# Attention heads between projection pairs: a hand-laid order on TensorE, and a low part formed from PSUM

## The chip, the cores and the metric

The kernel runs on one core of one Trainium2 chip. The metric is the device time of one execution in microseconds; three runs of the kernel before are compared by their median. TensorE (PE in the profile) multiplies matrices into PSUM, ScalarE (ACT), VectorE (DVE) and GpSimd (POOL) work elementwise, and SyncE (SP) issues the transfers. Each engine takes its own instructions in order and waits for others by semaphores.

## The reference

```
scores = scale * q @ k.T                       # 8 batches, 8 heads, 576 positions, 64 wide
mask_local   = (rel >= 0) & (rel < 32)         # heads 0 to 3
mask_strided = (rel >= 0) & (same position modulo 32)   # heads 4 to 7
attn = exp(scores - max) / (sum + 1e-9)
x = (attn @ v), heads side by side             # 4608 tokens x 512
h = max(x @ w_in, 0)                           # 512 -> 2048
out = (h * h) @ w_out                          # 2048 -> 512
```

All inputs and the output are float32.

## The kernel before

The 4608 tokens are worked off in 12 chunks of 384. For each chunk there are two parts: the attention that makes its x, and the two projections.

**Projections.** A slot is one sixteenth of the hidden width of one chunk, so there are 16 slots j in a chunk and 192 slots s in all. `up(c, j)` makes 128 hidden values for the 384 tokens: twelve matmuls of 384 columns into one bank of PSUM (line 430), because each product is split into high and low parts (high by high, high by low, low by high) over four pieces of the input width. The bank is one of three, in turn. ScalarE then applies Relu and Square in place (435, 436) and casts to the high part `gh` (437); VectorE subtracts that from the bank to get the low part `gl` (438). Both have two buffers, so `gh` of slot s waits until the down projection of slot s-2 has read its own. `down(c, j)` adds the slot's part of the output with nine matmuls of 512 columns (line 450) into three banks that stay open through the chunk; after the chunk's last slot they are copied out and stored. The slots are traced as up(s), then down(s-2), so two ups lie ahead of each down.

**Strided heads.** For the heads 4 to 7 of the later chunks GpSimd multiplies (380, 402) and VectorE sums (381, 403). TensorE takes no part.

**Local heads.** For the chunks 2 to 11, each of the four heads 0 to 3 is a generator, `pe_head`, with six stages, a `yield` after each:

- stage 0: two loads, q with k, and v (208, 209)
- stage 1: ScalarE casts k and q to a high part, GpSimd subtracts for the low part (214 to 217)
- stage 2: four score matmuls in two banks (231); VectorE adds the mask and takes the minimum (235, 223)
- stage 3: exponent on ScalarE (240), sums and reciprocal on VectorE, scaling (245 or 248)
- stage 4: v is split in parts (251, 252); VectorE transposes the probabilities (256) into `p_t`; ScalarE casts their high part (262) and VectorE subtracts for the low part (263), into `px`
- stage 5: four output matmuls in two banks (273); per bank ScalarE copies one third part out (276), VectorE adds the two others (277, 278); then x is cast and its low part made (280, 281)

The banks of the heads are `ps3` and `ps4`, dealt in turn by one counter, two calls in stage 2 and two in stage 5:

```
    def bank(nm):
        return psum(3 + next(turn) % 2, f"{nm}{u}")
```

A new tile of a bank waits until every reader of the tile before it is done.

**What sets the order.** Each engine's instructions are put in order when the program is built, by a planner that works with its own costs: it places what is ready by its own clock, with the order of the code as a guide. `tc.issue_after(ins)` ties the instructions traced inside it to come after `ins` on the engine of `ins`, in order of issue only, and binds no other engine. In the kernel before, the heads' stages for chunk c+1 are traced between the slots of chunk c by the function `local` and the counters `dl`, `fl`, and the planner chooses where their matmuls come among the projections. Chunks 0 and 1 have their local heads from another function, `pe_pair`. Weights are loaded and converted during chunk 0.

Of the kernel before, what the change touches and what calls it, by code (L numbers as in the profile page):

```python
# [17 lines left out]
HL = H // 2  # L18
# [5 lines left out]
TC = 384  # L24
WP = 512
NCHUNK = NT // TC
NFT = DF // P
# [57 lines left out]
def attn_moe(ctx: ExitStack, tc, qk_l, v_l, qk_d, v_d, qk_p, v_p, f_s, q_s, k_s, v_s, w_in, w_out, masks, eye, out):  # L85
# [107 lines left out]
    def pe_head(c, h):  # L193
        u = f"{c}_{h}"

        def bank(nm):
            return psum(3 + next(turn) % 2, f"{nm}{u}")

        def buf(pl, nm, n, tag, **kw):
            return pl.tile([P, n], F32, name=f"{nm}{u}", tag=tag, **kw)  # L200

        qk, vp = buf(lraw, "qk", TC + KC, "qk"), buf(lraw, "v", NW * D, "v")
        e = buf(lpool, "e", 512, "e")
        qr, kr = qk[:, :TC], qk[:, TC:]
        vr = vp.rearrange("p (w d) -> p w d", d=D)
        kw, wins = KW, [(at, 0 if qc == 0 else 1) for _, qc, at in windows(c)]
        nk = wins[-1][0] + KW
        nc.sync.dma_start(out=qk[:, : TC + nk], in_=qk_l[c, h, :, : TC + nk])
        last["s"] = nc.sync.dma_start(out=vp, in_=v_l[c, h])
        yield  # L210

        qx = lpool.tile([P, TC], F32R, name=f"qx{u}", tag="qh", bufs=1)
        kx = lpool.tile([P, 2, KC], F32R, name=f"kx{u}", tag="kx", bufs=1)
        nc.scalar.copy(kx[:, 0, :nk], kr[:, :nk])
        nc.gpsimd.tensor_sub(kx[:, 1, :nk], kr[:, :nk], f32(kx[:, 0, :nk]))  # L215
        nc.scalar.copy(qx, qr)
        nc.gpsimd.tensor_sub(qx[D:], qr[D:], f32(qx[D:]))
        yield
        nmax = small.tile([P, 2 * NW], F32, name=f"nm{u}", tag="nm")
        ssum = sums[h % 3]  # L220
        rs = small.tile([P, 2 * NW], F32, name=f"rs{u}", tag="rs")[:, :NW]
        cut = lambda w: slice(w * kw, (w + 1) * kw)
        reduce = lambda w, src, m: nc.vector.tensor_tensor_reduce(  # L223
            out=e[:QC, cut(w)], in0=src, in1=m, scale=-SCALE, scalar=3.0e38,
            op0=ALU.add, op1=ALU.min, accum_out=nmax[:QC, w : w + 1],
        )
        for a in range(0, NW, 2):
            s_ps = bank(f"s{a}")
            for w in (a, a + 1):
                k0 = wins[w][0]  # L230
                nc.tensor.matmul(s_ps[:QC, 256 * (w - a) : 256 * (w - a + 1)], qx[:, w * QC : (w + 1) * QC], kx[:, :, k0 : k0 + kw], start=True, stop=True)  # L231
            sv = s_ps[:QC].rearrange("p (w t k) -> p w t k", w=2, t=2)
            m = wins[a][1]
            ev = e[:QC, a * kw : (a + 2) * kw].rearrange("p (w k) -> p w k", w=2)
            nc.vector.tensor_add(ev, sv[:, :, 1, :], mask_sb[:QC, m : m + 2, :])
            for w in (a, a + 1):
                reduce(w, sv[:, w - a, 0, :], e[:QC, cut(w)])
        yield
        for w in range(NW):
            nc.scalar.activation(e[:QC, cut(w)], e[:QC, cut(w)], AF.Exp, bias=nmax[:QC, w : w + 1], scale=-1.0, accum_out=ssum[:QC, w, :1])  # L240
        nc.vector.tensor_reduce(out=rs[:QC], in_=ssum[:QC, :NW], op=ALU.add, axis=AX.X)
        nc.vector.reciprocal(rs[:QC], rs[:QC])
        if h != HL - 1:
            for w in range(NW):
                nc.scalar.mul(e[:QC, cut(w)], e[:QC, cut(w)], rs[:QC, w : w + 1])  # L245
        else:
            ew = e[:QC, : NW * kw].rearrange("p (w k) -> p w k", k=kw)
            last["g"] = nc.gpsimd.tensor_mul(ew, ew, rs[:QC].unsqueeze(2).broadcast_to([QC, NW, kw]))
        yield
        vx = lpool.tile([P, NW, 2, D], F32R, name=f"vx{u}", tag="vx", bufs=1)  # L250
        nc.scalar.copy(vx[:, :, 0, :], vr)
        nc.gpsimd.tensor_sub(vx[:, :, 1, :], vr, f32(vx[:, :, 0, :]))
        pt = p_t[h % 2]
        for r in range(QC // STR):
            for k in (r, r + 1):
                nc.vector.transpose(  # L256
                    out=pt[STR * k : STR * (k + 1), :, STR * r : STR * (r + 1)],
                    in_=e.rearrange("p (w k) -> p w k", k=KW)[STR * r : STR * (r + 1), :, STR * k : STR * (k + 1)],
                )
        src = pt.rearrange("p w q -> p (w q)")  # L260
        px = lpool.tile([P, 2, TC], F32R, name=f"px{u}", tag="px")
        nc.scalar.copy(px[:, 0, :], src)
        nc.vector.tensor_sub(px[:, 1, :], src, f32(px[:, 0, :]))  # L263
        yield
        x = x_tiles(c)
        par, hp = D * (h % 2), h // 2

        src = e[par : par + D, :TC]
        for a in range(0, NW, 2):
            o_ps = bank(f"o{a}")  # L270
            for w in (a, a + 1):
                sl = slice(w * QC, (w + 1) * QC)
                nc.tensor.matmul(o_ps[:, 2 * QC * (w - a) : 2 * QC * (w - a + 1)], vx[:, w].rearrange("p t d -> p (t d)"), px[:, :, sl], start=True, stop=True)  # L273
            ov = o_ps[:, : 4 * QC].rearrange("p (w t q) -> p w t q", w=2, t=2)
            part = src[:, a * QC : (a + 2) * QC].rearrange("p (w q) -> p w q", w=2)
            nc.scalar.copy(part, ov[D:, :, 0, :])
            nc.vector.tensor_add(part, ov[:D, :, 1, :], part)
            nc.vector.tensor_add(part, ov[:D, :, 0, :], part)
        dst = [x["l", s][par : par + D, hp, :] for s in "hl"]
        last["a"] = nc.scalar.copy(dst[0], src)  # L280
        last["g"] = nc.gpsimd.tensor_sub(dst[1], src, f32(dst[0]))
        yield
# [137 lines left out]
    def up(c, j):  # L420
        x = xt[c]
        p, o = divmod(j, 2)
        ph = psum(j % 2 if c == 0 else (c * NFT + j) % 3, f"h{c}_{j}")
        n = 0
        for kt in range(4):
            kind, kk = "ls"[kt // 2], kt % 2
            xh, xl = x[kind, "h"][:, kk, :], x[kind, "l"][:, kk, :]
            wsl = slice(kt * 256 + o * P, kt * 256 + (o + 1) * P)
            for w, xx in ((wi[p][0], xh), (wi[p][0], xl), (wi[p][1], xh)):
                nc.tensor.matmul(ph[:, :TC], w[:, wsl], xx, start=n == 0, stop=n == 11)  # L430
                n += 1
        gh = gpool.tile([P, TC], F32R, name=f"gh{c}_{j}", tag="gh")
        gl = gpool.tile([P, TC], F32R, name=f"gl{c}_{j}", tag="gl")
        g = ph[:, :TC]
        nc.scalar.activation(g, g, AF.Relu)  # L435
        nc.scalar.activation(g, g, AF.Square)  # L436
        nc.scalar.copy(gh, g)  # L437
        nc.vector.tensor_sub(gl, g, f32(gh))  # L438
        g_tiles[c, j] = gh, gl

    def down(c, j):
        gh, gl = g_tiles.pop((c, j))
# [4 lines left out]
        for t in range(NTT):  # L447
            sl = slice(t * P, (t + 1) * P)
            for k, (g, w) in enumerate(((gh, wo[p][0]), (gh, wo[p][1]), (gl, wo[p][0]))):
                nc.tensor.matmul(y_ps[c][t], g[:, sl], w[:, wsl], start=j == 0 and k == 0, stop=j == NFT - 1 and k == 2)  # L450
        if j == NFT - 1:
            for t in range(NTT):
                y = ypool.tile([P, DM], F32, name=f"ysb{c}_{t}", tag="ysb")
                (nc.scalar.copy if t == 1 else nc.vector.tensor_copy)(y, y_ps[c][t])
                nc.sync.dma_start(out=out[c * TC + t * P : c * TC + (t + 1) * P, :], in_=y)


    def run(gen):
# [37 lines left out]
        return pe_pair(c, pr, local, *b, bank, place % 3)  # L496

    def local(c):
        if c < NPLAIN:
            heads = [pair_at(c, pr, True, pr, "34") for pr in range(2)]  # L500
            turns = (0, 0, 1, 0, 1, 0, 0, 1, 1, 1)
        else:
            heads = [pe_head(c, h) for h in range(HL)]

            turns = [0] * 3
            for h in range(HL):
                turns += [h] + [h + 1] * (3 if h + 1 < HL else 0) + [h] * 2
        for h in turns:
            next(heads[h])
            yield  # L510

    ungated = convert()

# [50 lines left out]
    NS = NCHUNK * NFT  # L564
    for s in range(NS + 2):
        c, j = divmod(s, NFT)
        if s < NS:
            up(c, j)
        if s >= 2:
            down(*divmod(s - 2, NFT))  # L570
        if c == 0:
            for _ in range(WRATE):
                if next(weights, "end") != "end":
                    weights_end = {e: last[e] for e in "agsv"}
        if c + 1 < NCHUNK:
            if j == 0:
                lo, st = local(c + 1), strided(c + 1)
                if c == 0:
                    lo, st = behind(heads_end, lo), behind(heads_end, st)
                if c == 1:  # L580
                    lo, st = behind(weights_end, lo), behind(weights_end, st)
                cost = sum(2 * sum(range(i0 + 1, i1 + 1)) + 10 for _, i0, i1, _ in ranges(c + 1))
                dl = ds = 0
            fl, fs = ((j + 1) / n for n in SPREAD[min(c, 1)])
            while dl < fl * (10 if c + 1 < NPLAIN else 6 * HL) and next(lo, "end") != "end":
                dl += 1
            while ds < fs * cost:
                k = next(st, "end")
# [82 lines left out]
```

## Time and profile before

| | us |
|---|---|
| median of three runs | 903.63 (903.14 to 903.86) |
| profiled execution | 902.66 |
| its span, first to last instruction | 900.8 |
| TensorE busy | 886.3 (98%) |
| VectorE busy | 669.5 (74%) |
| GpSimd busy | 693.4 (77%) |
| ScalarE busy | 564.4 (63%) |

The mean granted clock of TensorE is 0.982 of full speed over the span. Rows of the profile are read like this. A row of the timeline has start, length, engine, line, operation, what is written from what, and how many such instructions were merged; in brackets the idle time before and what ended it. A row of the groups has busy time and mean length in ns, then the engine's idle time in front of the group. A row of the windows has the stretch, its length, then busy time and count for TensorE, its weight loads, VectorE, ScalarE and GpSimd, then the granted clock and the share and rate of the transfers. Matmul rows are longer than the distance at which matmuls follow each other, so that distance is read from start to start.

### The profile page before, as it was taken

Reading aid. Unit: us, or ns where it says so; the run is one execution under the profiler, and the core shown is the slowest. Engines: PE = TensorE matmul, PEld = TensorE weight load, DVE = VectorE, ACT = ScalarE, POOL = GpSimd, SP = SyncE. Lnnn points to the kernel's source line nnn. Section 1 sums busy time; section 2 is a strip of 40 time slices with the busy share of each in tenths; the row PEclk is TensorE's granted clock in tenths of the full one; section 3 lists DMA queues with packets and bytes.
Section 4 is the critical chain, followed back from the end, with each engine's and each line's share of the span. In section 5 each row is a group of like instructions: output and inputs, shape, how many; then the busy total and the mean of one; then the engine's idle time right before and its main releaser. Section 6 shows DMA issues by size and latency. Waiting matters only on the chain.

```text
span 900.8 us, 14866 instructions
## 1 busy us (share of the span) xinstructions
PE 886.3 (98%) x4744; PEld 800.0 (89%) x4744; DVE 669.5 (74%) x1840; ACT 564.4 (63%) x1458; POOL 693.4 (77%) x724
## 2 busy tenths in 40 slices
PE   8989999999999999999999999999999999999997
PEld 7778899999999999999989989999999999999996
DVE  6789668878877878878878887887886887885111
ACT  3898967657657657747746755755665765764332
POOL 5788577788788889989879997988899799785000
PEclk8599999999999999999999999999999999999999
DMA  9833441323113114102212311221131111000000
GB/s 352 346 123 126 129 150 35 121 69 104 51 51 112 47 48 139 43 13 98 75 32 69 104 31 54 59 86 60 28 110 47 46 46 68 25 1 2 35 1 35
DMA packets 26798, 71.41 MB, mean 79 GB/s; under 512 B 2976, under 2 KB 8736, under 8 KB 25184
## 3 DMA queue, kind: packets, MB, share of 16 engines
q1 hardware_dynamic: 26432, 70.14, 23.4%
q8 instruction: 37, 0.61, 0.3%
q10 hardware_dynamic: 288, 0.33, 0.1%
q14 instruction: 41, 0.34, 0.1%
HBM read 61.01 MB, written 9.44 MB: 78 GB/s over the span
## 4 chain that ended last, share of the span: by engine, by line
PE 86%; POOL 5%; DVE 5%; ACT 2%; issue 1%; DVEq 0%; POOLq 0%; ACTq 0%
PE h L430 41%; PE y L450 40%; POOL pp L402 2%; PE s L231 2%; PE o L273 2%; POOL pq L380 1%; DVE sc L381 1%; DVE px L263 1%; PE b L308 1%; DVE p_t L256 1%; PE w_ps L525 1%; PE b L335 0%; POOL kx L215 0%; DVE e L312 0%; DVE nm L313 0%
## 5 line engine op out<-in xcount | busy, mean ns | idle before, releaser
L450 PE MATMUL y<-w,gh 128*128 128x512 f32 x1152 | 361.9, 395 | 2.4 <-ACT gh L437 2.4
L450 PEld LDWEIGHTS y<-w,gh 128*128 128x128 f32 x1152 | 212.6, 189 | 35.0 <-ACT gh L437 2.6
L430 PE MATMUL h<-xlh,w 128*128 128x384 f32 x768 | 232.7, 342 | 0.4 <-DVE xsl L351 0.4
L430 PE MATMUL h<-xsh,w 128*128 128x384 f32 x768 | 228.1, 337 | 0.0
L402 POOL TENSOR_TENSOR pp<-vs,sc 128x448 f32<-128x448 f32 (+10 forms) x192 | 193.6, 1034 | 39.9 <-issue 21.7
L450 PE MATMUL y<-w,gl 128*128 128x512 f32 x576 | 223.7, 395 | 0.0
L380 POOL TENSOR_TENSOR pq<-ks,qs 128x512 f32<-128x512 f32 (+2 forms) x192 | 200.1, 1063 | 16.0 <-DVE sc L381 12.4
L381 DVE TENSOR_REDUCE sc<-pq 128x8 f32<-128x512 f32 (+4 forms) x228 | 120.1, 535 | 61.4 <-POOL pq L380 59.7
L435 ACT ACTIVATE h<-h 128x384 f32<-128x384 f32 x192 | 91.0, 475 | 112.6 <-PE h L430 111.5
L438 DVE TENSOR_TENSOR gl<-h,gh 128x384 fp32r<-128x384 f32 x192 | 105.4, 549 | 61.4 <-ACT gh L437 59.9
L430 PEld LDWEIGHTS h<-xlh,w 128*128 128x128 f32 x768 | 142.9, 189 | 8.4 <-DVE xsl L351 0.7
L430 PEld LDWEIGHTS h<-xsh,w 128*128 128x128 f32 x768 | 142.5, 189 | 0.5 <-ACT w L169 0.3
L403 DVE TENSOR_REDUCE qs<-pp 128x64 f32<-128x448 f32 (+11 forms) x192 | 106.8, 563 | 31.7 <-POOL pp L402 29.6
L430 PE MATMUL h<-xll,w 128*128 128x384 f32 x384 | 130.3, 339 | 0.0
L430 PE MATMUL h<-xsl,w 128*128 128x384 f32 x384 | 129.2, 336 | 0.0
L450 PEld LDWEIGHTS y<-w,gl 128*128 128x128 f32 x576 | 108.0, 188 | 20.8
L437 ACT CAST gh<-h 128x384 fp32r<-128x384 f32 x192 | 91.2, 475 | 34.1 <-PE y L450 30.3
L436 ACT ACTIVATE h<-h 128x384 f32<-128x384 f32 x192 | 91.0, 474 | 4.5
L240 ACT ACTIVATE e<-e,nm 96x128 f32<-96x128 f32 x160 | 62.6, 392 | 28.3 <-DVE nm L223 27.0
L430 PEld LDWEIGHTS h<-xll,w 128*128 128x128 f32 x384 | 72.8, 190 | 7.5
L256 DVE STREAM_TRANSPOSE p_t<-e 32x128 f32<-32x128 f32 x240 | 72.2, 301 | 4.8 <-ACT e L245 1.4
L430 PEld LDWEIGHTS h<-xsl,w 128*128 128x128 f32 x384 | 72.7, 189 | 0.2
(82 smaller groups left out, 1113.6 us busy)
## 6 DMA issues: line engine op xcount, KB each, us to landing
qk<-qk_l SPq DMA_DIRECT2D x24, 400.0 KB, 3.1
y<-ysb SPq DMA_DIRECT2D x36, 256.0 KB, 2.3
raw<-w_in SPq DMA_DIRECT2D x7, 1024.0 KB, 11.1
qk<-qk_l SPq DMA_DIRECT2D x16, 416.0 KB, 3.1
vs<-v_s SPq DMA_DIRECT2D x10, 576.0 KB, 3.8
raw<-w_out SPq DMA_DIRECT2D x5, 1024.0 KB, 13.3
v<-v_l SPq DMA_DIRECT2D x40, 128.0 KB, 2.0
ks<-k_s SPq DMA_DIRECT2D x8, 576.0 KB, 3.7
```

The source lines that it names most:

```text
L240: nc.scalar.activation(e[:QC, cut(w)], e[:QC, cut(w)], AF.Exp, bias=nmax[:QC, w : w + 1], scale=-1.0, accum_out=ssum[:QC, w, :1])
L256: nc.vector.transpose(out=pt[STR * k : STR * (k + 1), :, STR * r : STR * (r + 1)], in_=e.rearrange("p (w k) -> p w k", k=KW)[STR * r : STR ...
L380: nc.gpsimd.tensor_mul(pv, kt[:, a : a + m, :], qt[:, i - i0 : i - i0 + 1, :].broadcast_to([P, m, D]))
L381: nc.vector.tensor_reduce(out=sc[:, i - i0, a : a + m], in_=pv, op=ALU.add, axis=AX.X)
L402: nc.gpsimd.tensor_mul(pv, vt[:, a : a + nd, :n], sc[:, il : il + 1, :n].broadcast_to([P, nd, n]))
L403: nc.vector.tensor_reduce(out=ot[:, il, a : a + nd], in_=pv, op=ALU.add, axis=AX.X)
L430: nc.tensor.matmul(ph[:, :TC], w[:, wsl], xx, start=n == 0, stop=n == 11)
L435: nc.scalar.activation(g, g, AF.Relu)
L436: nc.scalar.activation(g, g, AF.Square)
L437: nc.scalar.copy(gh, g)
L438: nc.vector.tensor_sub(gl, g, f32(gh))
L450: nc.tensor.matmul(y_ps[c][t], g[:, sl], w[:, wsl], start=j == 0 and k == 0, stop=j == NFT - 1 and k == 2)
```

## The change

It has three parts.

- From the second chunk on, two slots are taken together, called a pair here: the ups of s and s+1, then the downs of s-2 and s-1. A chunk has eight pairs, 0 to 7. Each half of a pair is tied behind the last matmul before it. Chunk 0 keeps the old order.
- The stages of the heads of chunks 2 to 11 are called from a table, `plan`. For each pair it names the heads whose next stage comes before the ups, between ups and downs, and after the downs. The matmuls of a stage are tied behind the matmul before them, and what follows is tied behind them. Three stages of the next chunk's heads are called after pair 7.
- In stage 4 ScalarE also copies `p_t` into a bank of PSUM, and VectorE subtracts the high part from that copy rather than from `p_t`. The bank is the one that takes the first output matmuls of the head in stage 5, so it is drawn one stage earlier.

```
         px = lpool.tile([P, 2, TC], F32R, name=f"px{u}", tag="px")
+        o_ps = bank("o0")
+        nc.scalar.copy(o_ps[:, :TC], src)
         nc.scalar.copy(px[:, 0, :], src)
-        nc.vector.tensor_sub(px[:, 1, :], src, f32(px[:, 0, :]))
+        nc.vector.tensor_sub(px[:, 1, :], o_ps[:, :TC], f32(px[:, 0, :]))
         yield
...
         for a in range(0, NW, 2):
-            o_ps = bank(f"o{a}")
+            if a:
+                o_ps = bank(f"o{a}")
...
     def local(c):
-        if c < NPLAIN:
-            heads = [pair_at(c, pr, True, pr, "34") for pr in range(2)]
-            turns = (0, 0, 1, 0, 1, 0, 0, 1, 1, 1)
-        else:
-            heads = [pe_head(c, h) for h in range(HL)]
-
-            turns = [0] * 3
-            for h in range(HL):
-                turns += [h] + [h + 1] * (3 if h + 1 < HL else 0) + [h] * 2
-        for h in turns:
+        heads = [pair_at(c, pr, True, pr, "34") for pr in range(2)]
+        for h in (0, 0, 1, 0, 1, 0, 0, 1, 1, 1):
             next(heads[h])
             yield
+    heads = {}
+    plan = {
+        0: ("", "0", "01"),
+        1: ("", "1", "012"),
+        2: ("", "0", "123"),
+        3: ("", "12", "23"),
+        4: ("", "3", "23"),
+        5: ("", "2", "3"),
+        6: ("", "3", ""),
+        7: ("", "", ""),
+    }
+    def take(c, which):
+        if NPLAIN <= c < NCHUNK:
+            for h in map(int, which):
+                if (c, h) not in heads:
+                    heads[c, h] = pe_head(c, h)
+                with tc.issue_after(last["pe"].ins):
+                    last.pop("mm", None)
+                    next(heads[c, h])
+                    last["pe"] = last.get("mm", last["pe"])
...
     for s in range(NS + 2):
         c, j = divmod(s, NFT)
-        if s < NS:
+        if s < NFT:
             up(c, j)
-        if s >= 2:
-            down(*divmod(s - 2, NFT))
+            if s >= 2:
+                last["pe"] = down(*divmod(s - 2, NFT))
+        elif s % 2 == 0:
+            before, between, rest = plan[j // 2]
+            for part, slots, two in (up, (s, s + 1), before), (down, (s - 2, s - 1), between):
+                take(c + 1, two)
+                with tc.issue_after(last["pe"].ins):
+                    for i in slots:
+                        if 0 <= i < NS:
+                            last["mm"] = part(*divmod(i, NFT))
+                last["pe"] = last["mm"]
+            take(c + 1, rest)
+        if j == NFT - 2:
+            take(c + 2, "010")
...
-                lo, st = local(c + 1), strided(c + 1)
+                lo, st = local(c + 1) if c == 0 else iter(()), strided(c + 1)
```

The score and output matmuls, `up` and `down` now return or note their last matmul, so that the next step can be tied behind it. The local heads of chunk 2 are no longer held behind the end of the weights' conversion; its strided heads still are.

More of the change, by code (lines that the diff above doesn't have):

```diff
@@ L230, in pe_head @@
                 k0 = wins[w][0]
-                nc.tensor.matmul(s_ps[:QC, 256 * (w - a) : 256 * (w - a + 1)], qx[:, w * QC : (w + 1) * QC], kx[:, :, k0 : k0 + kw], start=True, stop=True)
+                last["mm"] = nc.tensor.matmul(s_ps[:QC, 256 * (w - a) : 256 * (w - a + 1)], qx[:, w * QC : (w + 1) * QC], kx[:, :, k0 : k0 + kw], start=True, stop=True)
             sv = s_ps[:QC].rearrange("p (w t k) -> p w t k", w=2, t=2)
@@ L269, in pe_head @@
         for a in range(0, NW, 2):
-            o_ps = bank(f"o{a}")
+            if a:
+                o_ps = bank(f"o{a}")
             for w in (a, a + 1):
                 sl = slice(w * QC, (w + 1) * QC)
-                nc.tensor.matmul(o_ps[:, 2 * QC * (w - a) : 2 * QC * (w - a + 1)], vx[:, w].rearrange("p t d -> p (t d)"), px[:, :, sl], start=True, stop=True)
+                last["mm"] = nc.tensor.matmul(o_ps[:, 2 * QC * (w - a) : 2 * QC * (w - a + 1)], vx[:, w].rearrange("p t d -> p (t d)"), px[:, :, sl], start=True, stop=True)
             ov = o_ps[:, : 4 * QC].rearrange("p (w t q) -> p w t q", w=2, t=2)
@@ L429, in up @@
             for w, xx in ((wi[p][0], xh), (wi[p][0], xl), (wi[p][1], xh)):
-                nc.tensor.matmul(ph[:, :TC], w[:, wsl], xx, start=n == 0, stop=n == 11)
+                done = nc.tensor.matmul(ph[:, :TC], w[:, wsl], xx, start=n == 0, stop=n == 11)
                 n += 1
@@ L439, in up @@
         g_tiles[c, j] = gh, gl
+        return done
     def down(c, j):
@@ L449, in down @@
             for k, (g, w) in enumerate(((gh, wo[p][0]), (gh, wo[p][1]), (gl, wo[p][0]))):
-                nc.tensor.matmul(y_ps[c][t], g[:, sl], w[:, wsl], start=j == 0 and k == 0, stop=j == NFT - 1 and k == 2)
+                done = nc.tensor.matmul(y_ps[c][t], g[:, sl], w[:, wsl], start=j == 0 and k == 0, stop=j == NFT - 1 and k == 2)
         if j == NFT - 1:
@@ L455, in down @@
                 nc.sync.dma_start(out=out[c * TC + t * P : c * TC + (t + 1) * P, :], in_=y)
+        return done
     def run(gen):
@@ L580, in attn_moe @@
                 if c == 1:
-                    lo, st = behind(weights_end, lo), behind(weights_end, st)
+                    st = behind(weights_end, st)
                 cost = sum(2 * sum(range(i0 + 1, i1 + 1)) + 10 for _, i0, i1, _ in ranges(c + 1))
@@ L584, in attn_moe @@
             fl, fs = ((j + 1) / n for n in SPREAD[min(c, 1)])
-            while dl < fl * (10 if c + 1 < NPLAIN else 6 * HL) and next(lo, "end") != "end":
+            while dl < fl * 10 and next(lo, "end") != "end":
                 dl += 1
```

## The prediction

> **What bounds the kernel now.** I read the page first: span, engine shares, granted clock.
>
> ```profile
> span 900.8 us, 14866 instructions
> PEclk8599999999999999999999999999999999999999
> ```
>
> The clock that TensorE is granted is full in nearly every slice. The waits, the windows and the chain are read next. The list of waits for TensorE says how little it stands still, the windows say what one chunk takes, and the chain that ended last gives the length of one down projection (nine `y` matmuls) and one up projection (twelve `h` matmuls).
>
> ```profile
> PE o L273 <- DVE px L263: 1.3, 1, 1.3
> 327.90:398.60 70.70, 70.70 (x370) 64.33 (x369) 57.14 (x166) 45.11 (x125) 62.42 (x63) 1.00 0.23 74
> 400.83 2.08 PE y L450 x9
> 402.91 2.10 PE h L430 x12
> 406.93 0.64 PE L231 MATMUL s<-kx,qx 128*96 128x256 f32 x4
> 407.41 0.34 PE L430 MATMUL h<-xlh,w 128*128 128x384 f32 x1
> 423.72 0.58 PE L273 MATMUL o<-px,vx 128*128 128x192 f32 x4
> 424.14 0.42 PE L450 MATMUL y<-w,gl 128*128 128x512 f32 x1
> ```
>
> From chunk 2 on, the list has one wait: 1.3 us, for a head's probabilities. A chunk takes 16 x (2.10 + 2.08) = 66.9 us of projections; a head costs 0.48 us of score matmuls (406.93 to 407.41) and 0.42 us of output matmuls (423.72 to 424.14), four heads 3.6. That makes 70.5 of the 70.7 us. So TensorE does its work back to back and the order changes none of it: after a down the next up starts without a gap. What the change can win is the 1.3 us wait and at most 0.2 us in each of ten chunks, 3.3 us in all. Any wait that it puts on TensorE is paid in full.
>
> **The new order, and the place where it waits.** The heads of chunks 2 to 11 are laid out by `plan`. Head 1 has its stages at: scores between ups and downs of pair 1, exponent after pair 1, probabilities after pair 2, outputs in pair 3. Head 2 has its scores in pair 3 too (`"12"`): TensorE must issue head 1's four output matmuls, then head 2's four score matmuls, then the two downs, each held behind the one before. The banks of the heads are two, 3 and 4, dealt in turn, and each head draws two for scores and two for outputs in the order of the code: scores of 0 (3, 4), scores of 1 (3, 4), outputs of 0 (3, 4), outputs of 1 (3, 4), scores of 2 (3, 4). So head 2's scores need the very banks that head 1's outputs have just filled, and these come free after a ScalarE copy and two VectorE adds each (lines 276 to 278). Behind the waiting scores stand the downs of the pair, and behind them everything. Elsewhere a bank is filled again half a pair or more after it was filled before.
>
> What the emptying costs, by an output group that ran as one piece in the kernel before, and one that ran in halves:
>
> ```profile
> 459.60 2.59 DVE L263 TENSOR_TENSOR px<-p_t,px 128x384 fp32r<-128x384 f32 x1
> 462.33 0.66 PE L273 MATMUL o<-px,vx 128*128 128x192 f32 x4
> 462.86 0.53 ACT L276 COPY e<-o 64x192 f32<-64x192 f32 x2 [1.97 <-PE o L273]
> 464.78 0.69 DVE L381 TENSOR_REDUCE sc<-pq 128x8 f32<-128x512 f32 x1 [0.82 <-POOL pq L380]
> 465.50 0.62 DVE L277 TENSOR_TENSOR e<-o,e 64x192 f32<-64x192 f32 x2
> 466.04 0.34 DVE L278 TENSOR_TENSOR e<-o,e 64x192 f32<-64x192 f32 x1
> 467.13 0.35 DVE L278 TENSOR_TENSOR e<-o,e 64x192 f32<-64x192 f32 x1
> 440.30 0.32 ACT L276 COPY e<-o 64x192 f32<-64x192 f32 x1 [0.15 <-PE o L273]
> 439.67 0.48 ACT L437 CAST gh<-h 128x384 fp32r<-128x384 f32 x1
> ```
>
> The group at 462.33 had its second bank free at 467.13 + 0.35 = 467.48, 5.15 us after its first matmul. TensorE restarts 0.14 us after VectorE is done (459.60 + 2.59 = 462.19, then 462.33). Of that it can use 0.42 us for the outputs and half of the scores, 0.24. Upper end: 5.15 + 0.14 - 0.66 = 4.6 us for each of ten chunks. Lower end, with nothing else in any queue: 0.53 to the start of the copy (462.33 to 462.86), 0.32 for one copy, 0.62 for the first two adds, 0.34 + 0.35 for the second two, 2.16 us; plus 0.14 less 0.66 is 1.64 us. I take a value nearer the lower end. In pair 3 VectorE has no other head's work: head 0 is done, head 1 has no transposes left, head 2 waits for these scores, and the `gl` of this pair waits for downs that stand behind the wait. What remains is the strided half, as in the row at 464.78: one sum of 0.69 ahead of an add. On ScalarE the second activation of the up that has just ended comes in ahead half the time (0.48, by the cast of that size): 0.24. 1.64 + 0.69 + 0.24 = 2.6 us, ten times: **+26 us** (16 to 46).
>
> **The clock after such a wait.** Two waits of the kernel before, and the stretch behind each:
>
> ```profile
> 45.30:48.70 3.40, 1.57 (x11) 1.11 (x10) 1.79 (x4) 3.27 (x9) 1.41 (x2) 1.00 0.22 54
> 48.70:52.10 3.40, 2.87 (x7) 2.30 (x8) 3.40 (x9) 2.57 (x6) 2.31 (x2) 0.50 0.19 73
> 530.00:533.40 3.40, 2.06 (x11) 1.51 (x10) 3.40 (x3) 1.82 (x5) 2.61 (x3) 1.00 0.13 39
> 533.40:536.80 3.40, 3.40 (x20) 3.18 (x20) 2.48 (x6) 1.89 (x5) 2.63 (x3) 1.00 0.00 0
> 49.23 2.93 PE L450 MATMUL y<-w,gh 128*128 128x512 f32 x6 [2.35 <-ACT gh L437]
> 405.01 2.08 PE y L450 x9
> ```
>
> After the wait of 2.35 us (busy 1.57 of 3.40 us) the granted clock was 0.50 in the next 3.4 us; after that of 1.34 us (busy 2.06) it stayed 1.00. Six `y` matmuls behind the first took 2.93 us; at 2.08 us for nine, six take 1.39, and with the drain of the last (0.40 of row length less 0.23 of pitch) 1.56: 1.37 us lost. A wait of 2.6 us, cut in two by a pair of scores, lies between the two cases but nearer the first. I count it 6 times in 10: **+8 us** (0 to 14). The Trainium skill, TensorE: Matmul & The Clock Gate, section on HAM oscillation, puts the limit at idle gaps of over some 3.4 us; by that rule no wait of 2.6 us would drop the clock and the sum would be 8 us lower. The trace disagrees: 2.35 us was enough in the stretch from 45.30.
>
> **Pairs of slots.** `up` takes its bank from a ring of three. The bank of an even slot s goes to up(s+3), and is free when `gl` of s is made, which waits for down(s-2) to release `gh`. In the old order down, up, down stood between (6.3 us at the rows above, and heads); now it is one down and one up, 4.18 us.
>
> ```profile
> 526.91 0.39 PE L450 MATMUL y<-w,gl 128*128 128x512 f32 x1
> 530.02 0.47 ACT L437 CAST gh<-h 128x384 fp32r<-128x384 f32 x1
> 532.95 0.55 DVE L438 TENSOR_TENSOR gl<-h,gh 128x384 fp32r<-128x384 f32 x1
> 465.28 0.48 ACT L437 CAST gh<-h 128x384 fp32r<-128x384 f32 x1 [0.45 <-PE y L450]
> 467.71 0.55 DVE L438 TENSOR_TENSOR gl<-h,gh 128x384 fp32r<-128x384 f32 x1
> ```
>
> The second took 2.98 us from the release (465.28) to 468.26, within 4.18. The first took from 527.14 to 533.50, 6.36 us: 2.2 too long. With one of that kind in each of ten chunks it costs 22 us, with none 0. I take **+4**: that one stood behind a `px` of 2.89 us (next part), which goes, and VectorE catches up during the new waits. The other ends get more room: the rows of a chunk's last down now have two ups instead of one before their banks are written again.
>
> **The low part by way of PSUM.** Forty copies are added on ScalarE and forty VectorE subtractions get one operand from PSUM instead of both from SBUF.
>
> ```profile
> L263 DVE TENSOR_TENSOR px<-p_t,px 128x384 fp32r<-128x384 f32 x40 | 39.1, 978 | 1.0 <-ACT px L262 0.8
> L438 DVE TENSOR_TENSOR gl<-h,gh 128x384 fp32r<-128x384 f32 x192 | 105.4, 549 | 61.4 <-ACT gh L437 59.9 <-PE h L430 0.3
> 530.14 2.89 DVE L263 TENSOR_TENSOR px<-p_t,px 128x384 fp32r<-128x384 f32 x1
> 516.21 0.41 PE L231 MATMUL s<-kx,qx 128*96 128x256 f32 x2
> 533.18 0.67 PE L273 MATMUL o<-px,vx 128*128 128x192 f32 x4 [1.34 <-DVE px L263]
> PE 886.3 (98%) x4744; PEld 800.0 (89%) x4744; DVE 669.5 (74%) x1840; ACT 564.4 (63%) x1458; POOL 693.4 (77%) x724
> ```
>
> The nearest row with one PSUM operand and the same shape is `gl`: 549 ns against 978. VectorE loses 40 x 0.43 = 17 us of work; ScalarE gains 40 x 0.48 = 19 us and stands at 65%. Neither sets the end, and the long `px` goes with its 1.34 us wait: **-1.5 us** with the small rest. The copy lengthens the way from scores to outputs by 0.5 us. The longest now runs from 516.21 to 533.03, 16.8 us, of which 2.3 are the long `px`; 15.0 remain, against two pairs, 2 x 8.36 = 16.7 us, and the heads' matmuls. It is hidden, with 2 us to spare; if the strided half pushes it out, the excess is TensorE's. The copy also takes the outputs' first bank one stage early and waits on ScalarE for the head before to leave it; `gh` stands behind that wait, and the 4 us above hold it.
>
> **Loads and casts** (two loads on SP, two casts, two POOL subtractions ahead of the scores) keep their number.
>
> ```profile
> qk<-qk_l SPq DMA_DIRECT2D x24, 400.0 KB, 3.1
> L215 POOL TENSOR_TENSOR kx<-qk,kx 128x416 fp32r<-128x416 f32 (+1 forms) x40 | 46.4, 1160 | 3.6 <-ACT kx L214 3.6
> L217 POOL TENSOR_TENSOR qx<-qk,qx 64x384 fp32r<-64x384 f32 x40 | 41.9, 1047 | 3.1
> ```
>
> 3.1 us to land, a cast of 0.5, 1.16 and 1.05 on POOL: 5.8 us. Heads 1 to 3 have a pair or more for it. Head 0's stand in the code after pair 7, with only the two ups of the next pair, 4.2 us, before its scores; but nothing ties SP, ScalarE or POOL to that place, and the buffers are free from pair 4 on. I take 0; if they did start only there, it would be 1.6 us in each chunk, 16 us. Behind a load that waits for its buffer on SP stand the strided half's loads, which POOL needs; POOL had 62.4 of 70.7 us busy and does not set the end. The last head is done in pair 6, earlier than before, and TensorE was not waiting there.
>
> **The sum**: 900.8 of span in an execution of 902.66 us; + 26 + 8 + 4 - 1.5 = 939.2. The median of three runs, 903.63, is 1 us above it: 940.
>
> **Rivals.** (1) Short waits: the planner puts the adds ahead and each costs 1.64 us, without a drop of the clock, as at 530 us: 903.6 + 16 + 2 - 1.5 = 920. For it: 440.30 shows ScalarE serving the copy at once behind a cast. (1b) Waits of 2.6 us with the clock at 1.00 after each, as at 533.4: 940 - 8 = 932. Against it: the row at 48.70. It is what the Trainium skill's rule, named above, would give. (2) Long waits, as at 462.33, each with the slow clock: 10 x (4.6 + 1.4) = 60, +8, -1.5: 970. Against it: less VectorE work in pair 3. (3) The ring of three becomes the main loss, 22 us in place of 4: 958. Against it: the rows at 465.28 and 467.71, 1.2 us inside the limit. (4) The other side: pairing takes out a loss hidden in TensorE's busy time. It can give back only the 0.2 us per chunk above and the one wait, 900 us; it decides only if the ten waits come to under 0.3 us each, below the 1.64 that the emptying alone takes. That needs TensorE not to be held, say because the scores end up in other banks than the order of the code gives, in which case the change also does not do what I read: 900 to 903.
>
> **How the numbers follow.** My case 45% (935 to 950), short waits 14%, full clock 9%, long waits 13%, the ring 8%, no wait 11%. The likeliest is 940. To hold 8 in 10 the range runs from the short waits, with a little less than the bare chain, to the long ones: 914 to 968. A measurement of this kernel tells 0.2%, 1.8 us, from no change. Faster by more: 0.07, the larger part of no wait; within: 0.04; slower: 0.89.
>
> **What would show it.** Right: the chain of waits has TensorE at the scores (line 231) on the second add about ten times, 2 to 3 us in total for each; the windows show a granted clock under 1.00 once a chunk; `px` falls to 0.55 us; `h` shows a few waits on `gl`; chunks of 73 to 75 us. Wrong: score matmuls that follow outputs without a gap, chunks of 70.5, or waits mainly at `h` or `o`.

## The result, and the profile after

The changed kernel takes 935.81 us (934.64 to 936.87) against 903.63, each the median of four runs: ratio 1.0357, 95% interval 1.0339 to 1.0374. Forecast were 940 us and a range of 914 to 968. The profiled execution took 936.34 us, with a span of 934.5.

The list of waits on TensorE in the changed kernel (what waited, for what, us in total, times, longest), and the group of its subtractions for `px`:

```profile
PE s L231 <- DVE e L282: 22.8, 15, 2.3
PE y L455 <- ACT gh L441: 6.5, 2, 5.8
PE h L434 <- DVE gl L442: 2.6, 2, 1.9
L266 DVE TENSOR_TENSOR px<-o,px 128x384 fp32r<-128x384 f32 x40 | 21.9, 548 | 2.3 <-ACT o L264 2.2
```

The one wait for `px` is gone, and the scores (line 231) wait 15 times for the second add behind the outputs (now line 282). One such place, first as TensorE ran it, then as the chain of waits saw it (its steps of 0.02 to 0.05 us called issue are left out):

```profile
521.93 0.58 PE L277 MATMUL o<-px,vx 128*128 128x192 f32 x4
524.00 0.45 PE L231 MATMUL s<-kx,qx 128*96 128x256 f32 x2 [1.49 <-DVE e L282]
525.10 0.45 PE L231 MATMUL s<-kx,qx 128*96 128x256 f32 x2 [0.65 <-DVE e L282]
...
522.13 0.45 ACT h L439
522.63 0.32 ACT e L280
522.97 0.61 DVE e L281 x2
523.59 0.27 DVE e L282
523.88 0.70 DVE sc L385
524.60 0.36 DVE e L282
524.96 0.14 issue
525.10 0.45 PE s L231 x2
525.55 4.58 PE y L455 x13
```

Four outputs take 0.42 us and two scores 0.24, so TensorE should have gone on at 521.93 + 0.42 = 522.35 and 524.00 + 0.24 = 524.24. It lost 524.00 - 522.35 = 1.65 and 525.10 - 524.24 = 0.86 us, 2.5 in this chunk. Counted so, from start to start, the ten chunks lost 1.7 to 3.2 us each, 25.5 in all (25.9 if two scores right behind a wait, which start 0.28 apart, are also charged the 0.04). The list has less because it counts from the ends of matmul rows, which overlap. In the chain stand the Relu of the up that has just ended, one copy, three adds, one sum of the strided half, the last add.

Windows, with length, busy time of TensorE (count) and, third from the end, the granted clock. The first two are two chunks; the others are two pairs, each a stretch with a wait at the scores and the stretch behind it:

```profile
343.90:418.60 74.70, 72.03 (x370) 65.38 (x369) 56.55 (x162) 46.11 (x128) 62.89 (x64) 0.98 0.20 67
418.60:491.50 72.90, 70.46 (x370) 64.26 (x369) 57.56 (x165) 46.12 (x128) 64.26 (x66) 1.00 0.20 63
153.50:156.90 3.40, 1.31 (x9) 1.11 (x8) 3.26 (x10) 2.57 (x7) 3.33 (x5) 1.00 0.09 29
156.90:160.30 3.40, 3.40 (x9) 2.63 (x9) 2.10 (x12) 2.58 (x11) 3.16 (x4) 0.50 0.03 10
597.20:600.60 3.40, 1.56 (x9) 1.40 (x10) 3.31 (x11) 2.37 (x6) 3.40 (x5) 1.00 0.12 36
600.60:604.00 3.40, 3.40 (x17) 2.85 (x16) 2.19 (x12) 2.88 (x13) 3.17 (x4) 1.00 0.01 3
```

The chunks 2 to 10, of 70.6 to 72.3 us before, became chunks of 72 to 75. Six of the ten waits at the scores were followed by 3.4 us of half clock. In those stretches 40 matmuls of `y` stand 0.43 us apart in place of 0.23, and nine more 0.26 to 0.40 apart, together as much as some 44 full ones: 44 x 0.196 = 8.6 us.

The account, by starts of matmuls in the two traces: scores 25.5, half clock 8.6, two waits for the ring of banks 3.0, the half clock behind the first of them 1.7 (half of 3.41 us without a gap, 132.99 to 136.40 us), the way to chunk 1's first up 2.8 (118.9 us against 116.1), the `px` wait -1.5, and matmuls that follow each other more closely, -6. That is 34.1 against 33.7 us of span.

### The profile page after: what moved, and what is told of

Same layout as the page of the kernel before. It is cut to its first block, busy times and chain, and to the rows that moved or that the text cites. A ratio compares the mean times of both kernels' runs of the same rounds, so it can differ in the third digit from the quotient of the medians.

```text
span 934.5 us, 14791 instructions
## 1 busy us (share of the span) xinstructions
PE 891.2 (95%) x4744; PEld 805.6 (86%) x4744; DVE 657.8 (70%) x1840; ACT 576.7 (62%) x1498; POOL 679.9 (73%) x724
## 4 chain that ended last, share of the span: by engine, by line
PE 82%; DVE 9%; POOL 4%; ACT 3%; issue 1%; DMA 0%; DVEq 0%; POOLq 0%; ACTq 0%
PE y L455 39%; PE h L434 38%; POOL pq L384 2%; PE s L231 2%; DVE sc L385 2%; DVE p_t L256 1%; PE o L277 1%; PE w_ps L548 1%; DVE e L281 1%; DVE e L282 1%; POOL pp L406 1%; DVE e L316 1%; DVE ysb L459 0%; DVE z L165 0%; DVE nm L317 0%
## 5 line engine op out<-in xcount | busy, mean ns | idle before, releaser
L455 PEld LDWEIGHTS y<-w,gh 128*128 128x128 f32 x1152 | 216.0, 193 | 48.4 <-ACT gh L441 6.9
L434 PE MATMUL h<-xlh,w 128*128 128x384 f32 x768 | 229.8, 340 | 3.1 <-DVE gl L442 2.6
L434 PE MATMUL h<-xsh,w 128*128 128x384 f32 x768 | 226.7, 335 | 0.0
L384 POOL TENSOR_TENSOR pq<-ks,qs 128x512 f32<-128x512 f32 (+2 forms) x192 | 197.1, 1045 | 26.6 <-DVE sc L385 22.2
L406 POOL TENSOR_TENSOR pp<-vs,sc 128x448 f32<-128x448 f32 (+10 forms) x192 | 189.1, 1012 | 28.6 <-DVE qs L407 11.5
L455 PEld LDWEIGHTS y<-w,gl 128*128 128x128 f32 x576 | 110.3, 192 | 23.3
L256 DVE STREAM_TRANSPOSE p_t<-e 32x128 f32<-32x128 f32 x240 | 72.3, 301 | 12.5 <-ACT e L245 7.6
L434 PEld LDWEIGHTS h<-xsl,w 128*128 128x128 f32 x384 | 72.3, 188 | 0.4 <-DVE xsl L355 0.4
```

Source lines behind the costliest of these rows:

```text
L256: nc.vector.transpose(out=pt[STR * k : STR * (k + 1), :, STR * r : STR * (r + 1)], in_=e.rearrange("p (w k) -> p w k", k=KW)[STR * r : STR ...
L384: nc.gpsimd.tensor_mul(pv, kt[:, a : a + m, :], qt[:, i - i0 : i - i0 + 1, :].broadcast_to([P, m, D]))
L406: nc.gpsimd.tensor_mul(pv, vt[:, a : a + nd, :n], sc[:, il : il + 1, :n].broadcast_to([P, nd, n]))
L434: done = nc.tensor.matmul(ph[:, :TC], w[:, wsl], xx, start=n == 0, stop=n == 11)
L455: done = nc.tensor.matmul(y_ps[c][t], g[:, sl], w[:, wsl], start=j == 0 and k == 0, stop=j == NFT - 1 and k == 2)
```

## The experiments

**Scores half a pair later.**

```
-        3: ("", "12", "23"),
-        4: ("", "3", "23"),
-        5: ("", "2", "3"),
-        6: ("", "3", ""),
+        3: ("", "1", "223"),
+        4: ("", "", "323"),
+        5: ("", "", "23"),
+        6: ("", "", "3"),
```

> Head 2's scores stand behind the two downs of pair 3 instead of right behind head 1's outputs, and what follows them stands half a pair later too; nothing else of the change is touched. Theory (TensorE waits for the two banks that the outputs have just filled, and its clock drops behind the wait): the 25.5 us at the scores and the 8.6 us of half-clock matmuls go, 935.8 - 34 = 902, and the waits have no line of the scores any more. Rival (pairs, ring of three banks or the table itself cost the time): over 925.

Measured: 900.27 us, ratio to before 0.9967 (0.9956 to 0.9977), 1.7 us below the sum expected. The list of waits has no scores any more:

```profile
PE y L455 <- ACT gh L441: 5.1, 2, 4.4
PE h L434 <- DVE gl L442: 1.9, 1, 1.9
```

Head 2's scores half a pair too early were worth 35 us, and without that the change is faster than the kernel before. Pairs and the ring of three banks are still there, so the loss did not come from them.

**The clock by itself.** Nine matmuls that nobody reads, behind head 1's outputs:

```
+        with tc.issue_after(last["pe"].ins):
+            f_ps = psum((c * NFT + 8) % 3, f"f{c}")
+            for i in range(NFILL):
+                last["pe"] = nc.tensor.matmul(f_ps[:, :TC], wi[0][0][:, :P], xt[c]["l", "h"][:, 0, :], start=True, stop=True)
```

> The changed kernel with nine matmuls of 384 columns, whose result nobody reads, between head 1's outputs and head 2's scores: TensorE works 1.6 us of the wait away. Theory (the clock drops because TensorE stands still there): the banks come free as late as before, the time at the scores that is left is under 1.5 us in each chunk, the clock stays at 1.00, 935.8 - 8.6 = 927. Rival (the drops do not hang on these waits, or the halved clock is hidden): 935 to 937; if the emptying itself is slowed by it: over 937.

Measured: 926.29 us, ratio 1.0255 (1.0241 to 1.0269), 9.5 less than the changed kernel. The timeline of TensorE in the filled kernel:

```profile
516.10 0.59 PE L278 MATMUL o<-px,vx 128*128 128x192 f32 x4
516.52 1.78 PE L530 MATMUL f<-xlh,w 128*128 128x384 f32 x9
518.17 0.45 PE L232 MATMUL s<-kx,qx 128*96 128x256 f32 x2
519.27 0.45 PE L232 MATMUL s<-kx,qx 128*96 128x256 f32 x2 [0.65 <-DVE e L283]
519.56 0.62 PE L456 MATMUL y<-w,gh 128*128 128x512 f32 x2
```

The scores started 2.07 and 3.17 us after the first output, as in the changed kernel, so the banks came free as late as before; TensorE worked for most of that time, and the clock stayed at 1.00 behind all ten waits. So the half clock hangs on TensorE standing still there, and is paid on top of the wait. Not all of the 9.5 us is from there: the first wait at the ring (still 2.0 us) was not followed by half clock in this trace either, and the second was gone.

**A shorter emptying.** The changed kernel without this line:

```
-            nc.vector.tensor_add(part, ov[:D, :, 0, :], part)
```

> The changed kernel without the second of the two VectorE adds per output bank (the product of the two high parts is left out of x). Theory (the wait is for the adds that empty the two banks): by the rows of 522 us the second bank is then free 0.3 us after the first and both about 1.3 us earlier, so the time lost at the scores falls from 2.55 to some 1.2 to 1.5 us in each of ten chunks; waits of that length left the clock at 1.00, so the 8.6 us of half clock go too: 912 to 918. Rival (the copy on ScalarE, or what stands before it, sets the wait): no line of the adds left, over 925. If the clock drops behind such waits as well: 921 to 924.

Measured: 913.41 us, ratio 1.0110 (1.0096 to 1.0124). The place of above:

```profile
508.77 0.58 PE L277 MATMUL o<-px,vx 128*128 128x192 f32 x4
510.22 0.74 PE L231 MATMUL s<-kx,qx 128*96 128x256 f32 x4 [0.87 <-DVE e L281]
PE s L231 <- DVE e L281: 10.7, 11, 1.6
```

One wait of 1.0 us (510.22 less 508.77 + 0.42 = 509.19) in place of two with 2.5. The longest of the ten waits from start to start was 1.8 us, and none was followed by half clock. Without the second adds about half of the wait is gone, 13 us in place of 25.5 in the ten chunks; the rest is for the copy and the first adds.

**Pairs alone.** The kernel before, with the pairs in its main loop and nothing else:

```
+        elif s % 2 == 0:
+            for part, slots in (up, (s, s + 1)), (down, (s - 2, s - 1)):
+                with tc.issue_after(last["pe"].ins):
...
```

> The kernel before with pairs of slots alone; the heads' stages are called and placed as before, and the low part is formed from SBUF. Theory: pairs gain, since the second up and the second down of a pair run at 2.083 and 2.043 us against 2.11 and 2.085, 0.08 us in each of 88 pairs, 7 us; with up to 3 us for the ring of three banks 897 to 901. Rival (the ring of three banks is the main loss of the change): over 920. The prediction's bound (nothing is hidden in TensorE's busy time): 903 to 907.

Measured: 905.89 us, ratio 1.0026 (1.0016 to 1.0036). The number fits the prediction's bound, but its reason does not hold: the second downs of the pairs took 2.043 us in this trace too, and the gain was lost to new waits, which no theory had, and to 6.8 us of half clock behind the longest (from 827.5 us):

```profile
PE h L430 <- ACT xsh L413: 3.8, 1, 3.8
PE h L430 <- POOL xsl L414: 2.1, 2, 1.3
```

With the heads left to the planner, the strided x of the last chunks came too late. Theory and rival missed; why the planner's order made it late was not tried.

**The copy in PSUM alone**, in the kernel before (the diff is that of the change).

> The kernel before with the copy in PSUM alone. Theory: the subtraction falls from 978 to 550 ns and the one wait for it, 1.3 us, goes; TensorE waits for nothing else, so 902 to 903. Rival (the longer way from scores to outputs and the bank held a stage longer cost time): 906 or more.

Measured: 901.58 us, ratio 0.9980 (0.9971 to 0.9989). From chunk 1 on no matmul of TensorE started more than 0.1 us late. This part is worth 1.8 us; 1.5 were forecast.

**Chunk 2's first stages tied.** Moving the scores left one loss unexplained: in chunk 0 TensorE waits for `gh` 6.5 us in all in the changed kernel and 5.1 in the shifted one, against 2.4 before. ScalarE in the changed kernel, then in the kernel before, in chunk 0:

```profile
47.99 0.84 ACT L440 ACTIVATE h<-h 128x384 f32<-128x384 f32 x2
48.77 0.55 ACT L214 CAST kx<-qk 128x448 fp32r<-128x448 f32 x1
49.22 0.51 ACT L216 CAST qx<-qk 128x384 fp32r<-128x384 f32 x1
49.64 0.47 ACT L441 CAST gh<-h 128x384 fp32r<-128x384 f32 x1
...
47.92 0.85 ACT L436 ACTIVATE h<-h 128x384 f32<-128x384 f32 x2
48.69 0.48 ACT L437 CAST gh<-h 128x384 fp32r<-128x384 f32 x1
```

The change had dropped the tie that held chunk 2's heads behind the weights, and head 0's casts went ahead of the first `gh`, which TensorE was waiting for. The first down started at 50.16 us in place of 49.23, 0.93 later, about what the two casts take (48.77 to 49.64); the list shows a longer wait because TensorE had done other work earlier. Behind it the clock stayed at half for two stretches, where the kernel before had one (48.71 to 52.12):

```profile
47.66:54.49 6.83, 4.33 (x12) 3.78 (x13) 6.83 (x14) 6.11 (x13) 6.58 (x6) 0.50 0.18 57
```

With the scores' shift kept, the tie is put back (the tied kernel from here on):

```
         if j == NFT - 2:
-            take(c + 2, "010")
+            with ExitStack() as tied:
+                for i in weights_end.values() if c == 0 else ():
+                    tied.enter_context(tc.issue_after(i.ins))
+                take(c + 2, "010")
```

> The shift by half a pair, and chunk 2's first three stages (two pairs of loads, head 0's casts) tied behind the weight conversions done by then, on ScalarE, VectorE, GpSimd and SyncE. Theory (untied, head 0's casts of 0.55 and 0.51 us went ahead of the first gh casts in chunk 0, and TensorE lost 2.1 us at its first down and 0.8 us at 62 us): 900.3 - 2 to 3 = 897 to 898.5. Rival (the longer first wait is the state of the start, loads or the planner's order, not the casts): 899.5 to 901.

Measured: 896.40 us, ratio 0.9922 (0.9908 to 0.9935): the fastest version, 0.8% ahead of the kernel before and 0.6 us below the range expected. Its waits and a chunk:

```profile
PE y L455 <- ACT gh L441: 2.4, 1, 2.4
PE h L434 <- DVE gl L442: 1.7, 1, 1.7
328.50:398.50 70.00, 70.00 (x369) 64.09 (x368) 56.10 (x163) 46.13 (x127) 62.49 (x65) 1.00 0.23 74
```

Head 0's casts now run at 113 us, the first down starts at 49.36 us, and half clock lasts one stretch again. The tie holds loads and the work of GpSimd as well as the casts, so what is shown is the worth of the tie, 3.9 us against the shifted kernel, and not of the casts alone.

The same tie in the changed kernel, scores left where they were:

> The changed kernel with chunk 2's first stages tied behind the weight conversions, nothing else. Theory (the untied casts cost the start 2 to 4 us, apart from the waits at the scores): 932 to 934, with a first wait for gh of 2.4 us again; the scores still wait 23 us. Rival (the start differs for another reason): 935 to 937.

Measured: 928.62 us, ratio 1.0278 (1.0261 to 1.0296), 3.4 us below the range of the theory, so neither expectation holds. The waits for `gh` went from two of 6.5 us in all to one of 3.3, chunk 1 began at 117.0 us in place of 118.9, five waits at the scores in place of six were followed by half clock, none at the ring was, and the waits at the scores came to 23.7 us from start to start. The planner had another order for every chunk, so not all of the 7.2 us are the tie's.

**Single slots at the same points.** The tied kernel with up, down, up, down:

```
-            for part, slots, two in (up, (s, s + 1), before), (down, (s - 2, s - 1), between):
+            for part, slots, two in (up, (s,), before), (down, (s - 2,), ""), (up, (s + 1,), between), (down, (s - 1,), ""):
```

> As the tied kernel, but up, down, up, down in place of up, up, down, down; the heads' matmuls at the same points but for the scores and outputs of the column between, which come ahead of the second up. Theory (a stream of matmuls of one width is slowed for its first microsecond, or longer, after the other width): second ups and second downs run at 2.11 and 2.085 again, 0.08 x 88 = 7 us more than the tied kernel, 904 to 906. Rival (the pairs' faster matmuls come from something else, such as the heads' placing): within 1.5 us of the tied kernel.

Measured: 903.28 us, ratio 0.9996 (0.9987 to 1.0005), 6.9 us more than with pairs, as expected in the difference though 0.7 us below the range. The chain that ended last, first with pairs (two ups, two downs), then single:

```profile
390.37 4.21 PE h L434 x24
394.58 4.12 PE y L455 x18
...
392.89 2.13 PE h L434 x12
395.01 2.08 PE y L455 x9
397.10 2.10 PE h L434 x12
```

After chunk 0 this kernel's list has one wait for the ring, of 1.5 us, and the tied one's has one of 1.7: the difference is not in waits but in the pairs' matmuls. Counted from start to start after chunk 0, the ups and downs take 12.6 us more than 173.3 and 226.7 ns a matmul with single slots, and 6.0 with pairs.

**One width.** The kernel with single slots, its downs cut to 384 columns:

```
-        wsl = slice(o * DM, (o + 1) * DM)
+        wsl = slice(o * DM, o * DM + TC)
```

> As the kernel with single slots, but each down projection makes only 384 of the 512 output columns (the other 128 are left out), so that ups and downs have matmuls of one width. Theory (the slow first matmuls of a slot come from the change of width): ups take 12 x 173.3 = 2.08 us and downs 9 x 173.3 = 1.56, without the pattern 178, 174, 177, 183 ns. Rival (they come from the switch between the two kinds of work, whatever the width): the pattern stays, ups take 2.11.

One execution: 877.0 us. With its shorter downs TensorE waits for the strided half, so the time tells nothing. The chain in a stretch without waits does:

```profile
781.67 1.56 PE y L455 x9
783.23 2.08 PE h L434 x12
785.31 1.56 PE y L455 x9
```

Ups of 2.08 us between downs of the same width, 2.10 to 2.13 between wider ones, and downs at 0.173 us a matmul throughout. The switch between the two kinds of work is still there and the slow matmuls are not, so they come with the change of width, as the theory has it.

**The tied kernel with the low part from SBUF.**

> As the tied kernel with the low part formed from SBUF, as before the change. Theory (the subtraction of 978 ns is hidden but for single long ones): 0 to 2 us more than the tied kernel, with one or two waits of the outputs for px. Rival (with the heads at set points the shorter subtraction is needed): waits of the outputs for px in most chunks, 5 us or more.

Measured: 901.33 us, ratio 0.9975 (0.9965 to 0.9986), 4.9 more than the tied kernel. Neither expectation holds. The outputs never waited for `px`; the mean subtraction was 922 ns against 546, and TensorE lost some 2 us at scores behind slower emptying. But chunk 1 also began 1.6 us later, and other gaps came with another order of the planner. How much of the 4.9 us is the subtraction stays open. This run also limits what was said of the start: the tie is in place and the casts stand at 115 us, yet TensorE waits 5.0 us for the first `gh` and the half clock lasts two stretches again (48.5 to 55.3 us). So the planner's order can bring that about without the casts.

## Why the prediction was right, and where it was not

- **The place and the chain.** Right: the banks, the pair, the emptying, and that it is paid in full; moving the scores gave it all back. The 26 us measured 25.5. On ScalarE, though, it was not Square half the time (0.24) but the Relu each time, with Square after the copy; it put the copy 0.70 us after the first output (521.93 to 522.63) where 0.53 was taken, so it cost 0.17 in all ten places. A strided sum stood between the adds in nine of the ten (0.70 in the one shown); the tenth, at 817.86 us, had none and lost 1.7 us, close to the 1.64 of the bare chain.
- **The clock.** Right in size, 6 in 10 and 8.6 us for 8, and the filled kernel shows the cause. The count of six was an interpolation between two waits; which of the ten waits fell was decided by how the grid of 3.41 us (last section) cut them, which the prediction did not have, so that the count came out exactly is luck. The limit that the Trainium skill names (TensorE: Matmul & The Clock Gate, HAM oscillation), idle gaps of over some 3.4 us, is too high for this case: a wait of 2.3 us brought the clock down, and so did one of 1.85 us at the ring (131.79 us).
- **The ring of three.** 3.0 us for 4, in two waits, not spread over the chunks; the half clock behind the first, 1.7 us, was not in the sum.
- **The copy in PSUM.** Right: -1.5 forecast, -1.8 alone; the subtraction went to 548 ns on average in the changed kernel.
- **"What the change can win is ... 3.3 us in all."** This step failed, and rival 4 with it. It took 2.10 and 2.08 us from the chain as work that the order cannot change, but those rows held the loss that pairs take out: 12 matmuls at 173.3 ns are 2.08, nine at 227 are 2.04. Pairs were worth 6.9 us, and the tied kernel ends below the 900 us that were said to be the floor. The remark that "the next up starts without a gap" was true and not enough: the gap is zero and the first matmuls are longer.
- **Loads and casts at 0.** The price of starting late was bounded, that of starting early was not. The dropped tie let casts go ahead of `gh` in chunk 0, and chunk 1 began 2.8 us later: 0.93 for the first down, most of the rest a second stretch of half clock. Putting the tie back was worth 3.9 us in the shifted kernel; how much of that is the casts and how much the planner's other order stays open.

The last two, -6 and +3, partly cancelled, so that 940 lay nearer than its steps deserved.

## What to carry to other kernels

When an engine is the bound, look for two steps side by side in its queue that share a buffer: the second waits for the whole emptying of the first, and other work between them hides it (here two downs, 4.1 us). Busy rows are no floor: compare the distance of like instructions in a row with that behind a switch. A table that fixes one engine's order leaves the others free, and a tie that is dropped along the way lets early work push ahead of what is urgent.

## What the runs showed of the hardware

Matmuls of 512 columns right behind others of that width followed each other at 227 ns, and those of 384 columns at 173. Behind a change of width the first six of 384 took 171 to 185 ns, 178 on average, and those of 512 224 to 236, 231 on average, through all nine (means by position in the changed kernel); with one width this was gone.

The granted clock changed on a grid of 3.41 us, and half clock came behind a stretch of the grid in which TensorE had done little. How long it waited in one piece does not decide it: a wait of 2.5 us that the grid split (596 us) cost no clock and one of 2.3 us (153 us) did. Nor does the busy time of the rows, since they count the modelled ends of matmuls too: 1.26 and 1.31 us busy were followed by half clock (522.1 and 153.5 us in the changed kernel), and 1.56 us was once (129.57) and once not (597.2).

```profile
522.10:525.50 3.40, 1.26 (x9) 0.92 (x9) 2.94 (x8) 2.39 (x6) 3.40 (x4) 1.00 0.00 0
525.50:528.90 3.40, 3.40 (x10) 2.62 (x9) 2.36 (x11) 2.12 (x8) 3.24 (x4) 0.50 0.13 39
129.57:132.99 3.42, 1.56 (x10) 1.25 (x9) 3.39 (x9) 1.58 (x4) 2.37 (x2) 1.00 0.33 128
132.99:136.40 3.41, 3.41 (x13) 3.27 (x12) 1.75 (x5) 1.21 (x3) 2.51 (x3) 0.50 0.00 0
```

Counted by starts, with each matmul at its usual distance, the two stretches of 1.56 us differ: TensorE was at work 1.27 us of the one from 129.57 and 1.48 us of the one from 597.2. By that count every stretch of the changed kernel after chunk 0 that was followed by half clock held at most 1.34 us of work, and every other one at least 1.48. That limit is an estimate, from the starts in one trace.
